# A new set of planning tables for a gated Fourier-mix and squared-ReLU MLP kernel

## Chip, cores and metric

The kernel runs on one core of a Trainium2 chip. The metric is the device time of one launch in microseconds (us). The median of three runs of the kernel before is 1730.49 us (1730.0 to 1730.5).

## What is computed

With x of 2048 rows and 1024 columns, the reference is, cut to its core:

```
g = sigmoid((x * gate_w).sum(-1, keepdims=True))
a = x @ Wd_re.T ;  b = x @ Wd_im.T                # hidden DFT, 1024 x 1024
y = Ws_re @ a - Ws_im @ b                         # sequence DFT, 2048 x 2048
h = x @ w1 + b1 ; h = where(h > 0, h, 0) ; h = h * h   # 1024 -> 3584
o = h @ w2 + b2                                   # 3584 -> 1024
out = g * y + (1 - g) * o
```

All of it is in float32.

## The kernel before

**Products.** Each of the large products is cut by a seven-product scheme (Strassen's in Winograd's form): sums of blocks ("S1" to "S4" of the left operand, "T1" to "T4" of the right, tables `SUMS_L`, `SUMS_R` and their kin) go in, seven smaller products come out, and their results are added up. For most of the seven the scheme is applied a second time (`twice`); the rest run as they are (`direct`). Each float32 operand is split into a high part `hi`, which ScalarE (ACT) writes by a copy, and a low remainder `lo`, which VectorE (DVE) writes by a subtraction; a block product is three matmuls, `hi*hi`, `lo*hi` and `hi*lo`. Narrow right operands keep both parts in one tile called `both`.

**Stages.** `x_stage` makes a and b (tiles `ab`), `c_stage` the sequence DFT (tiles `y`, stored in `gy` or in `out`), `h_stage` twice the hidden layer (tiles `h`, sums of them stored under the names `T`), `o_stage` the second layer, the gate and the last addition (tiles `o`). Sums of blocks are made by DVE (tiles `sum`, or in place in a loaded `raw` tile), or by an adding DMA from the POOL queue (`accum_op=ADD`), as the tables `LAND_*` say; `lo` can also be made by an adding DMA from a negated copy (`minus`, tables `MINUS_*`), and stored operands can be fetched again (`LOW`, `HIGH`: stores `lo<-lo`, `hi<-hi` by POOL, loads of the same names by SP).

**PSUM.** A `Group` owns one or two of four pools of PSUM, each a tile `ps` of 128 x 2 x 512 float32. In `x_stage` each block product is 24 matmuls: twelve into one pool, twelve into the next. After them DVE adds the pool's contents to a tile `ab` (an eviction), and the pool can be written again. The second-level order of the products in `twice` of a `wide` stage is

```
late = TURNS >> (0 if not flip else flip) & 1
...
if late:
    order = (1, chain), (5, other), (6, chain), (3, other), (7, chain), (2, last), (4, chain)
else:
    order = (*(begin if steps and "T1" not in ontos else begin[::-1]), (3, other), (6, chain), (2, last),
             (7, chain), (4, chain))
```

where `chain`, `other` and `last` are the groups that a product is accumulated in, and bit 0 of `TURNS` is for `x_stage`.

**Order.** The functions above only record operations. `plan` then gives each a due time by its table of costs, hands out 55 slots of SBUF (512 KB each) by due time less a lead (`LEAD`, and per 25 us of due time `LEADS`), and writes one order per engine: PE in program order, the others by due time as the planner expects them to be ready. `PATIENT` lets a POOL DMA be held back behind a later instruction (`op.gate`). `emit` issues the operations in that order; line 1628, where it does so, is the line of nearly every row of the profile. The gate's sixteen row sums (`Gate`, DVE `raw<-raw,gwb`) are placed by `GATE`, relative to the first step of `c_stage`.

Of the kernel before, what the change touches and what calls it, by code (L numbers as in the profile page):

```python
# [4 lines left out]

# [11 lines left out]
S, D, F = 2048, 1024, 3584
NF = F // P
SLOTS = 55
WIDE, TALL_C, TALL_O = (1, 2, 5, 6, 3, 7, 4), (1, 2, 5, 6, 3, 7, 4), (1, 2, 5, 6, 3, 7, 4)  # L20
WIDE_H = ((1, 2, 5, 6, 3, 7, 4), (1, 2, 5, 6, 3, 7, 4))
TWICE_X, TWICE_C, TWICE_O = (2, 3, 4, 5), {1: 4, 2: 4, 3: 4, 4: 4, 5: 2, 6: 1}, {1: 2, 2: 3, 3: 3, 4: 3, 5: 3, 7: 1}
FIRST_C, FIRST_O = {5: 2}, {7: 2}
WARM = 44
FAR_TALL, FAR_WIDE = ("T2",), ()
LAND_X, LAND_C, LAND_H, LAND_O = {'T1': 3, 'T3': 4, 'T4': 3}, {'T1': 15, 'T3': 0, 'T4': 13}, ({'T1': 0, 'T3': 4, 'T4': 3}, {'T1': 0, 'T3': 1, 'T4': 1}), {'T1': 10, 'T3': 3, 'T4': 9}
SHARE = ("S1", "S2", "S3", "S4")
NEAR_O = ("T1",)
ADD_O = range(13)
GATE, ROWS = (-44, 1), (14, 11)  # L30
OLD_X, OLD_H = (2, 6, 4), ((3, 4, 7, 6), (6, 4, 2))
SHARE2 = {1: 7, 2: 11, 3: 15, 4: 4, 5: 8, 6: 2, 7: 2}
LOW, HIGH = ({1: 111, 2: 49, 3: 109, 4: 119, 5: 32, 6: 63, 7: 36}, {1: 35, 2: 27, 3: 125, 4: 100, 5: 76, 6: 101, 7: 56}), ({1: 78, 2: 4, 3: 4, 5: 16, 6: 9, 7: 78}, {1: 33, 2: 50, 3: 41, 4: 67, 5: 4, 6: 101, 7: 19})
SPILL, LAND_CL = (1, 0), {'S1': 0, 'S2': 0, 'S3': 0, 'S4': 5}
# [24 lines left out]
ADD, SUB = ALU.add, ALU.subtract

# [9 lines left out]
LESS, LESS_C = {2: 1, 3: 1, 4: -1, 6: -1}, {2: -1, 3: -1, 4: 1, 6: -1}  # L70
# [9 lines left out]
def gated_mix_kernel(ctx: ExitStack, tc: tile.TileContext, x4, xn, w4, ct, w1a, w1b, w2, b1, b2, gw, out):  # L80
# [930 lines left out]
    def wide(left, right, rows, order, second, target, final, sign=1, onto_old=(), flip=False, lands={},  # L1011
# [143 lines left out]
    def x_stage():  # L1155
# [17 lines left out]
        def spill(c, k, near=None, lent=False):  # L1173
# [5 lines left out]
            if near is not None:  # L1179
# [136 lines left out]
    def o_stage():  # L1316
# [141 lines left out]
def plan(ops, count, start):  # L1458

    t = start  # L1460
# [32 lines left out]
    events, now, order = [], 0.0, []  # L1493
# [97 lines left out]
    while events:  # L1591
        now, _, _, what = heappop(events)
# [88 lines left out]
```

## Time and profile before

| what | value |
|---|---|
| median of three runs | 1730.49 us |
| profiled execution, first to last instruction (span) | 1727.9 us |
| PE busy | 1722.6 us (100%) |
| PE weight loads busy | 1508.7 us (87%) |
| DVE busy | 1658.3 us (96%) |
| ACT busy | 1151.2 us (67%) |
| POOL busy | 284.3 us (16%) |
| DMA: bytes, mean rate | 559.89 MB, 324 GB/s |

The profile gives the span of one execution, and no whole time of its own for it; the median of the runs is 2.6 us above the span. Busy times overlap: an engine with a share of 100% never rests, and one with less costs nothing by its rests as long as no other engine waits for it. Matmul starts are measured, their ends are modelled. As nearly all instructions have line 1628, groups are told apart by their tile names (`lo<-raw,hi` writes a `lo` tile from a `raw` and a `hi`).

### The profile page before, as it was taken

What the parts mean: (1) busy time and instruction counts of PE and PEld (TensorE: products, weight loads), DVE (VectorE), ACT (ScalarE), POOL (GpSimd) and SP (SyncE); (2) the same over time, 40 slices, a digit from 0 to 9 for tenths busy, and PEclk for the clock granted to TensorE, in tenths of its full rate; (3) what the DMA queues carried; (4) which work ended last, traced back from release to release, by engine and by line L of the source; (5) the groups of instructions that cost most, each with busy time, mean ns of one, the idle gap of its engine ahead of it and who ended that gap; (6) DMA issues with size and microseconds to landing.
All of it is one profiled execution on the core that took longest, in us unless ns stands there. A gap on an engine that the chain in (4) does not pass through costs nothing.

```text
span 1727.9 us, 22479 instructions
## 1 busy us (share of the span) xinstructions
PE 1722.6 (100%) x8024; PEld 1508.7 (87%) x8024; DVE 1658.3 (96%) x1659; ACT 1151.2 (67%) x1296; POOL 284.3 (16%) x413
## 2 busy tenths in 40 slices
PE   9999999999999999999999999999999999999999
PEld 8888888888888888888888888888888888888888
DVE  7999999999999899899999999999999999899997
ACT  5475565874675675466595668987897666476673
POOL 1212221111211100121121210101211120111131
PEclk9999999999999999999999999999999999999999
DMA  9996999999999999998998999999999999999997
GB/s 347 365 375 259 322 387 343 292 285 327 285 307 352 291 310 399 323 295 285 371 359 311 276 355 344 351 379 358 309 345 324 336 272 381 341 277 334 334 295 162
DMA packets 157807, 559.89 MB, mean 324 GB/s; under 512 B 17776, under 2 KB 18304, under 8 KB 157696
## 3 DMA queue, kind: packets, MB, share of 16 engines
q1 hardware_dynamic: 98352, 351.07, 52.9%
q0 software_dynamic: 58912, 207.00, 44.4%
q8 instruction: 63, 1.03, 0.2%
q10 hardware_dynamic: 432, 0.39, 0.1%
q14 instruction: 48, 0.39, 0.1%
HBM read 390.09 MB, written 134.75 MB: 304 GB/s over the span
## 4 chain that ended last, share of the span: by engine, by line
PE 96%; DVE 3%; DMA 1%; issue 0%; ACT 0%; DVEq 0%; POOLq 0%
PE ps L1628 96%; DVE lo L1628 1%; DVE sum L1628 1%; DMA raw<-in_w1a 1%; DVE y L1628 0%; DVE both L1628 0%; DVE u L1628 0%; DVE raw L1628 0%; ACT hi L1628 0%; ACT y L1628 0%; DVE o L1628 0%; ACT both L1628 0%; ACT ps L1628 0%; DVE ones L1628 0%; DVEq L1628 0%
## 5 line engine op out<-in xcount | busy, mean ns | idle before, releaser
L1628 PE MATMUL ps<-hi,lo 128*128 128x512 f32 (+1 forms) x2100 | 730.4, 378 | 0.1
L1628 PE MATMUL ps<-hi 128*128 128x512 f32 (+1 forms) x2100 | 730.4, 378 | 0.0
L1628 PE MATMUL ps<-lo,hi 128*128 128x512 f32 (+1 forms) x2100 | 730.3, 378 | 0.0
L1628 ACT ACTIVATE hi<-raw 128x1024 fp32r<-128x1024 f32 (+2 forms) x397 | 401.5, 1032 | 200.2 <-DVE raw L1628 79.6
L1628 PEld LDWEIGHTS ps<-hi,lo 128*128 128x128 f32 x2100 | 396.6, 189 | 56.5 <-DVE lo L1628 0.7
L1628 PEld LDWEIGHTS ps<-lo,hi 128*128 128x128 f32 x2100 | 396.7, 189 | 56.1 <-DVE lo L1628 0.2
L1628 PEld LDWEIGHTS ps<-hi 128*128 128x128 f32 x2100 | 396.6, 189 | 56.0 <-ACT hi L1628 0.2
L1628 DVE TENSOR_TENSOR lo<-raw,hi 128x1024 fp32r<-128x1024 f32 (+2 forms) x337 | 396.0, 1192 | 14.2 <-ACT hi L1628 10.8
L1628 ACT ACTIVATE hi<-sum 128x1024 fp32r<-128x1024 f32 (+1 forms) x263 | 269.1, 1032 | 136.7 <-DVE sum L1628 88.1
L1628 PE MATMUL ps<-hi,both 128*128 128x512 f32 x1120 | 312.3, 379 | 0.0
L1628 DVE TENSOR_TENSOR lo<-sum,hi 128x1024 fp32r<-128x1024 f32 (+1 forms) x230 | 270.5, 1191 | 8.7 <-PE ps L1628 4.6
L1628 PEld LDWEIGHTS ps<-hi,both 128*128 128x128 f32 x1120 | 211.7, 189 | 30.2 <-ACT ps L1628 0.2
L1628 DVE TENSOR_TENSOR raw<-raw 128x1024 f32<-128x1024 f32 (+1 forms) x175 | 205.7, 1195 | 1.6 <-DMA raw<-in_ct 0.5
L1628 DVE TENSOR_TENSOR sum<-raw 128x1024 f32<-128x1024 f32 (+2 forms) x182 | 180.5, 1002 | 7.9 <-PE ps L1628 4.4
L1628 PE MATMUL ps<-lo,both 128*128 128x512 f32 x560 | 182.9, 379 | 0.0
L1628 DVE TENSOR_TENSOR sum<-raw,sum 128x1024 f32<-128x1024 f32 (+2 forms) x139 | 147.6, 1066 | 4.4 <-DMA raw<-copy 2.1
L1628 ACT ACTIVATE u<-ps 128x1024 f32<-128x1024 f32 (+1 forms) x91 | 88.1, 970 | 47.5 <-PE ps L1628 28.0
L1628 PEld LDWEIGHTS ps<-lo,both 128*128 128x128 f32 x560 | 105.8, 189 | 15.0
L1628 ACT ACTIVATE ps<-u 128x1024 f32<-128x1024 f32 (+1 forms) x69 | 67.8, 987 | 21.9 <-DVE u L1628 9.5
L1628 POOL DMA_DIRECT2D h<-h x58 | 31.3, 542 | 250.5 <-ACT h L1628 91.0
L1628 POOL DMA_DIRECT2D lo<-raw x38 | 34.0, 896 | 224.9 <-ACT lo L1628 172.1
L1628 ACT ACTIVATE both<-sum 128x512 fp32r<-128x512 f32 x68 | 42.3, 622 | 35.9 <-DVE sum L1628 33.7
(87 smaller groups left out, 1140.0 us busy)
## 6 DMA issues: line engine op xcount, KB each, us to landing
raw<-in_ct SPq DMA_DIRECT2D x137, 512.0 KB, 10.1
raw<-h SPq DMA_DIRECT2D x99, 512.0 KB, 10.5
raw<-in_w SPq DMA_DIRECT2D x90, 512.0 KB, 10.3
raw<-ab SPq DMA_DIRECT2D x72, 512.0 KB, 10.9
raw<-copy SPq DMA_DIRECT2D x65, 512.0 KB, 7.8
raw<-in_x SPq DMA_DIRECT2D x56, 512.0 KB, 8.4
copy<-raw POOLq DMA_DIRECT2D x48, 512.0 KB, 6.9
h<-h POOLq DMA_DIRECT2D x44, 512.0 KB, 6.6
```

What stands on the lines that cost most here:

```text
L1628: made = getattr(real[op.engine], op.name)(*(actual(a) for a in op.args), **{k: actual(v) for k, v in op.kwargs.items()})
```

## The change

The arithmetic functions are the same. New are the values of the tables that decide which sums an adding DMA makes, which operands are stored and fetched, where the gate's sums stand, and how early a slot is handed out; and the planner's event heap now breaks ties by a counter instead of by an object's address. Cut to what is spoken of (a long table is cut in its line, at "..."):

```
-LAND_X, LAND_C, LAND_H, LAND_O = {'T1': 3, 'T3': 4, 'T4': 3}, {'T1': 15, 'T3': 0, 'T4': 13}, ...
+LAND_X = {'T1': 3, 'T3': 2, 'T4': 3}
+LAND_C = {'T1': 16, 'T3': 1, 'T4': 13}
...
-GATE, ROWS = (-44, 1), (14, 11)
+GATE = (-39, 1)
+ROWS = (14, 13)
...
-LOW, HIGH = ({1: 111, 2: 49, 3: 109, ...
+LOW = ({1: 47, 2: 49, 3: 109, 4: 119, 5: 32, 6: 63, 7: 36}, {1: 35, 2: 27, 3: 125, 4: 102, 5: 76, 6: 101, 7: 58})
...
-MINUS_C, MINUS_O = {1: 4227074, 2: 24661, ...
+MINUS_C = {1: 4227074, 2: 1610637397, 3: 30694026, 4: 285213248, 5: 151060480, 6: 59966531, 7: 2532114496}
...
-HIGH_FIRST, BEGIN2, TURNS, SPREAD = 26, 1, 7, 1
+HIGH_FIRST = 26
+BEGIN2 = 1
+TURNS = 6
+SPREAD = 1
...
-LEADS = {'hi': {3: -5.5, 4: -4.5, 7: 2.0, 10: 1.5, ...
+LEADS = {'hi': {1: -8.5, 2: 14.0, 3: 2.0, 4: -0.5, 5: -3.5, ...
...
+    turn = count_up()
+
     def push(t, *what):
-        heappush(events, (t, len(events) + 1e-9 * len(order), id(what), what))
+        heappush(events, (t, next(turn), 0, what))
```

By engine the built programs hold: PE 7,980 float32 matmuls in both; DVE one instruction more than before; ACT three fewer; plain loads and stores from SP and ACT 686 before and 687 now; DMAs from POOL 409 and 407, of them 169 and 166 adding ones.

**First place: PE in `x_stage`.** `TURNS` = 6 clears the bit of `x_stage`. The rows below are the first matmul of each run of twelve, from the 205th to the 277th float32 matmul; `ps_N` is a pool of PSUM in use by one group. Before:

```order
L1628 MATMUL ps_934<-hi_635,hi_645 128x512
...
L1628 MATMUL ps_954<-hi_731,hi_703 128x512
...
L1628 MATMUL ps_975<-hi_731,hi_703 128x512
...
L1628 MATMUL ps_905<-hi_759,hi_713 128x512
...
L1628 MATMUL ps_934<-hi_759,hi_713 128x512
...
L1628 MATMUL ps_954<-hi_751,hi_796 128x512
...
L1628 MATMUL ps_975<-hi_751,hi_796 128x512
```

Now:

```order
L1672 MATMUL ps_931<-hi_635,hi_646 128x512
...
L1672 MATMUL ps_950<-hi_765,hi_754 128x512
...
L1672 MATMUL ps_968<-hi_765,hi_754 128x512
...
L1672 MATMUL ps_950<-hi_700,hi_788 128x512
...
L1672 MATMUL ps_968<-hi_700,hi_788 128x512
...
L1672 MATMUL ps_906<-hi_743,hi_775 128x512
...
L1672 MATMUL ps_931<-hi_743,hi_775 128x512
```

Before, two pairs of pools take turns; now the pair `ps_950`, `ps_968` is written again as soon as its first product is done (at the 241st and the 253rd matmul). The same is new at the 337th, 349th, 505th, 517th, 877th, 1225th and 1237th: nine matmuls wait for an eviction that has twelve matmuls' time. Outside the 241st to the 1248th matmul PE's order is as it was.

**DVE at the same place.** The rows run from the eviction of the pool written before that pair. Before:

```order
L1628 TENSOR_TENSOR ab_959<-u_695,ps_934 128x1024
L1628 TENSOR_TENSOR lo_966<-sum_922,hi_944 128x1024
L1628 TENSOR_TENSOR lo_973<-raw_600,hi_956 128x1024
L1628 TENSOR_TENSOR ab_983<-u_804,ps_954 128x1024
L1628 TENSOR_TENSOR raw_864<-raw_864,raw_870 128x1024
L1628 TENSOR_TENSOR ab_1004<-u_826,ps_975 128x1024
L1628 TENSOR_TENSOR lo_1015<-raw_840,hi_988 128x1024
```

Now:

```order
L1672 TENSOR_TENSOR ab_957<-u_692,ps_931 128x1024
L1672 TENSOR_TENSOR sum_964<-raw_778,raw_790 128x1024
L1672 TENSOR_TENSOR ab_973<-u_811,ps_950 128x1024
L1672 TENSOR_TENSOR sum_983<-raw_624,raw_829 128x1024
L1672 TENSOR_TENSOR ab_997<-u_841,ps_968 128x1024
L1672 TENSOR_TENSOR lo_1006<-sum_964,hi_977 128x1024
L1672 TENSOR_TENSOR lo_1013<-sum_983,hi_1002 128x1024
```

One instruction instead of two stands ahead of the eviction of the pair's first pool; one stands between the two evictions, as before.

**Second place: POOL at the change from `c_stage` to `h_stage`.** An adding DMA onto a tile `raw` from `in_w1a`, and the stores behind it. Before:

```order
L1628 DMA raw_7183<-in_w1a 128x1024 [waits DMAHW4_49,DMASW0_49,DMAHW5_49,DVE_49,Activation_49]
L1628 DMA copy_426<-sum_7386 128x1024 [waits DMASW1_49,Activation_49]
L1628 DMA hi_428<-hi_7396 128x1024 [waits DMASW2_49,Activation_49]
L1628 DMA lo_427<-lo_7417 128x1024 [waits DMASW3_49]
L1628 DMA copy_429<-sum_7462 128x1024 [waits DMASW4_49,DVE_49]
```

Now:

```order
L1672 DMA raw_7167<-in_w1a 128x1024 [waits DMASW6_49,DMAHW4_49,DVE_49,Activation_49]
L1672 DMA copy_424<-sum_7385 128x1024 [waits DMASW7_49,DVE_49]
L1672 DMA hi_426<-hi_7396 128x1024 [waits DMASW0_49,Activation_49]
L1672 DMA lo_425<-lo_7417 128x1024 [waits DMASW1_49]
L1672 DMA copy_427<-sum_7463 128x1024 [waits DMASW2_49,DVE_49]
```

The order of the five is the same. What moved is what the third waits for: before, the store of `hi_7396` was held until a later ACT copy (the one that writes `hi` from the `raw` tile of `copy_364`) was done; now it waits for its own tile alone. The store of `lo` behind it comes free with it.

## Rows read from the trace of the kernel before

**Rows 1.** The page: span, and busy time with share and count by engine.

```profile
span 1727.9 us, 22479 instructions
PE 1722.6 (100%) x8024; PEld 1508.7 (87%) x8024; DVE 1658.3 (96%) x1659; ACT 1151.2 (67%) x1296; POOL 284.3 (16%) x413
PEclk9999999999999999999999999999999999999999
```

**Rows 2.** Windows of 50 us: PE, PEld, DVE, ACT, POOL busy (count), PEclk, DMA share, GB/s.

```profile
50.00:100.00 50.00, 50.00 (x234) 43.77 (x233) 48.60 (x48) 22.72 (x23) 8.22 (x14) 1.00 1.03 373
100.00:150.00 50.00, 50.00 (x234) 43.77 (x233) 50.00 (x49) 35.00 (x38) 9.04 (x17) 1.00 0.82 322
...
800.00:850.00 50.00, 49.85 (x231) 43.36 (x230) 48.94 (x44) 35.58 (x37) 7.76 (x12) 1.00 0.96 334
```

**Rows 3.** Groups by form: count | busy us, mean ns | idle before.

```profile
L1628 PE MATMUL ps<-hi,lo 128*128 128x512 f32 x2084 | 726.7, 379 | 0.1
L1628 PE MATMUL ps<-hi,both 128*128 128x512 f32 x1120 | 312.3, 379 | 0.0
L1628 PE MATMUL ps<-lo,both 128*128 128x512 f32 x560 | 182.9, 379 | 0.0
L1628 PE MATMUL ps<-hi 128*128 128x256 f32 x16 | 3.9, 274 | 0.0
L1628 PEld LDWEIGHTS ps<-hi,lo 128*128 128x128 f32 x2100 | 396.6, 189 | 56.5 <-DVE lo L1628 0.7
```

**Rows 4.** Timeline of PE: start, duration (us), instruction; first matmul, one stretch, last.

```profile
5.69 0.70 PE L1628 MATMUL ps<-hi 128*128 128x512 f32 x2
...
54.81 0.38 PE L1628 MATMUL ps<-hi,lo 128*128 128x512 f32 x1
55.03 0.38 PE L1628 MATMUL ps<-hi 128*128 128x512 f32 x1
...
1723.57 0.28 PE L1628 MATMUL ps<-hi,lo 128*128 128x256 f32 x1
```

**Rows 5.** Timeline of PE around 827 us.

```profile
827.16 0.38 PE L1628 MATMUL ps<-lo,hi 128*128 128x512 f32 x1
827.69 0.48 PE L1628 MATMUL ps<-hi,lo 128*128 128x512 f32 x1
828.01 0.38 PE L1628 MATMUL ps<-hi 128*128 128x512 f32 x1
```

**Rows 6.** Timeline of DVE in `x_stage`; in brackets idle time before, and its releaser.

```profile
53.08 1.21 DVE L1628 TENSOR_TENSOR ab<-u,ps 128x1024 f32<-128x1024 f32 x1
55.69 1.23 DVE L1628 TENSOR_TENSOR lo<-sum,hi 128x1024 fp32r<-128x1024 f32 x1 [1.40 <-ACT hi L1628]
...
57.97 1.22 DVE L1628 TENSOR_TENSOR ab<-u,ps 128x1024 f32<-128x1024 f32 x1
...
84.07 1.21 DVE L1628 TENSOR_TENSOR ab<-u,ps 128x1024 f32<-128x1024 f32 x1
```

**Rows 7.** The chain that ended last, in order of time, ahead of 827.69 us.

```profile
815.91 9.39 DMA raw<-in_w1a
...
825.32 1.06 ACT hi L1628
...
826.41 1.24 DVE lo L1628
827.64 0.04 issue
```

**Rows 8.** Timeline of POOL, 814 to 830 us.

```profile
817.48 0.57 POOL L1628 DMA_DIRECT2D copy<-sum  x1 [0.66 <-ACT hi L1628]
829.51 0.53 POOL L1628 DMA_DIRECT2D hi<-hi  x1 [11.46 <-ACT hi L1628]
```

**Rows 9.** Window 810 to 820 us: columns as in the windows above.

```profile
810.00:820.00 10.00, 10.00 (x48) 8.77 (x47) 10.00 (x10) 8.87 (x11) 1.48 (x2) 1.00 1.00 350
```

**Rows 10.** Timeline of DVE: its last instruction.

```profile
1724.40 0.43 DVE L1628 TENSOR_TENSOR o<-o,raw 128x256 f32<-128x256 f32 x1
```

More of the change, by code (lines that the diff above doesn't have):

```diff
@@ L3 @@
 from heapq import heappop, heappush
-from itertools import cycle, zip_longest
+from itertools import count as count_up, cycle, zip_longest
 import concourse.bass as bass
@@ L16 @@
 P = 128
[L17 removed]
+S = 2048
+D = 1024
+F = 3584
 NF = F // P
 SLOTS = 55
[L20 removed]
+WIDE = (1, 2, 5, 6, 3, 7, 4)
+TALL_C = (1, 2, 5, 6, 3, 7, 4)
+TALL_O = (1, 2, 5, 6, 3, 7, 4)
 WIDE_H = ((1, 2, 5, 6, 3, 7, 4), (1, 2, 5, 6, 3, 7, 4))
[L22 to L25 removed]
@@ L26 @@
-LAND_X, LAND_C, LAND_H, LAND_O = {'T1': 3, 'T3': 4, 'T4': 3}, {'T1': 15, 'T3': 0, 'T4': 13}, ({'T1': 0, 'T3': 4, 'T4': 3}, {'T1': 0, 'T3': 1, 'T4': 1}), {'T1': 10, 'T3': 3, 'T4': 9}
+TWICE_X = (2, 3, 4, 5)
+TWICE_C = {1: 4, 2: 4, 3: 4, 4: 4, 5: 2, 6: 1}
+TWICE_O = {1: 2, 2: 3, 3: 3, 4: 3, 5: 3, 7: 1}
+FIRST_C = {5: 2}
+FIRST_O = {7: 2}
+WARM = 44
+FAR_TALL = ("T2",)
+FAR_WIDE = ()
+LAND_X = {'T1': 3, 'T3': 2, 'T4': 3}
+LAND_C = {'T1': 16, 'T3': 1, 'T4': 13}
+LAND_H = ({'T1': 0, 'T3': 4, 'T4': 4}, {'T1': 0, 'T3': 1, 'T4': 3})
@@ L27 @@
+LAND_O = {'T1': 10, 'T3': 3, 'T4': 9}
 SHARE = ("S1", "S2", "S3", "S4")
 NEAR_O = ("T1",)
-ADD_O = range(13)
-GATE, ROWS = (-44, 1), (14, 11)
[L31 to L34, printed above, removed]
@@ L36 @@
-MADE = {'T1': 6884, 'T3': 14556}
-TWICE_H = ((1, 2, 5, 3, 4, 6, 7), (1, 2, 5, 3, 4, 6))
-MM, MM_END, FIRST_MM = 0.2157, 0.18, 6.2
-VEC, VEC_END, ACT, ACT_END = (0.07, 1.0417e-3), 0.39, (0.09, 0.843e-3, 0.04, 0.095), 0.41
-ADDING = 0.85, 2.1, 2.2
-ISSUE, RING, RATE, SEM, LANES = {'gpsimd': 0.56, 'scalar': 0.36, 'sync': 0.36}, {'gpsimd': (1.6, 1.6), 'scalar': (1.8, 1.8), 'sync': (1.8, 1.8)}, (420000.0, 395000.0), 0.06, 8
+ADD_O = range(0, 14)
+GATE = (-39, 1)
+ROWS = (14, 13)
+OLD_X = (2, 6, 4)
+OLD_H = ((3, 4, 7, 6), (6, 4, 2))
@@ new lines @@
+LAND2_H = ({1: ('T3',), 2: ('T3',), 3: ('T3',), 4: ('T1',), 5: ('T1',), 6: ('T1',), 7: ('T1',)}, {1: (), 2: (), 3: (), 4: (), 5: (), 6: ('T3', 'T1'), 7: ('T3', 'T1')})
+LAND2_O = {1: {'T1': 1, 'T3': 0}, 2: {'T1': 1}, 3: {'T3': 3}, 4: {'T3': 1}, 5: {'T1': 3, 'T3': 2}, 6: {'T1': 2}, 7: {'T1': 3, 'T3': 4}}
+MADE = {'T1': 6884, 'T3': 14552}
+TWICE_H = ((1, 2, 5, 3, 4, 6, 7), (1, 2, 5, 3, 4, 6))
+MM = 0.2157
+MM_END = 0.18
+FIRST_MM = 6.2
+VEC = (0.07, 1.0417e-3)
+VEC_END = 0.39
+ACT = (0.09, 0.843e-3, 0.04, 0.095)
@@ L43 @@
+ACT_END = 0.41
+ADDING = 0.85, 2.1, 2.2
+ISSUE = {'gpsimd': 0.56, 'scalar': 0.36, 'sync': 0.36}
+RING = {'gpsimd': (1.6, 1.6), 'scalar': (1.8, 1.8), 'sync': (1.8, 1.8)}
+RATE = (420000.0, 395000.0)
+SEM = 0.06
+LANES = 8
 RUN = {768: 0.75, 512: 0.6}
-EARLY_C, EARLY_O = 17172, 47911
+EARLY_C = 19120
+EARLY_O = 45373
 SQUARE = ((), ())
-NOW_C, NOW_O = (384, 17152, 12816), (12930, 4736, 6144)
-APART_C, APART_O = (640, 63815), (35458, 26362)
-MINUS_C, MINUS_O = {1: 4227074, 2: 24661, 3: 30694026, 4: 16777792, 5: 151060480, 6: 26936387, 7: 116195392}, {1: 205653010, 2: 8983296, 3: 67907648, 4: 93114368, 5: 42107932, 6: 243963922, 7: 30949506}
@@ L56 @@
+MINUS_O = {1: 232914962, 2: 67703552, 3: 67907648, 4: 76042496, 5: 42106904, 6: 243963922, 7: 155992194}
+RELU = ((), (3,))
+TWINS_C = 1
+TWINS_O = 3
+BOTH_C = 20720
+BOTH_O = 6718
+HIGH_FIRST = 26
+BEGIN2 = 1
+TURNS = 6
+SPREAD = 1
+BY_ROW_C = 251
+BY_ROW_O = 56
+BEGIN = 1
+OUT = 15
+NOT_OUT = ((0, 0, 1, 0), (0, 1, 0, 0), (0, 1, 1, 1), (1, 0, 1, 0), (1, 1, 0, 1), (1, 1, 1, 0))
+LATE = 720.0
+PATIENT = (32.0, 0)
 LEAD = {'hi': 2.2, 'out': 1.4, 'raw': 6.7, 'sum': 10.0}
-LEADS = {'hi': {3: -5.5, 4: -4.5, 7: 2.0, 10: 1.5, 11: -1.0, 15: -3.0, 16: -6.0, 18: 2.0, 19: 5.5, 20: 7.5, 25: -0.5, 29: -4.5, 30: -9.5, 31: -2.5, 37: 4.5, 38: -0.5, 40: -1.0, 41: 3.5, 42: 2.5, 43: -3.0, 44: -7.0, 45: 1.0, 47: 0.5, 50: -1.0, 54: -5.0, 61: -1.0, 62: -2.0, 64: -2.0}, 'out': {9: -2.0, 12: 3.0, 15: -3.0, 17: -1.5, 25: 5.5, 34: -2.0, 41: -0.5, 45: 2.0, 49: -8.0, 55: 3.0, 56: 6.5, 65: 4.0}, 'raw': {3: -1.0, 10: 2.0, 11: -2.0, 13: 1.0, 14: 4.5, 16: 1.5, 17: 4.5, 18: 7.5, 19: 7.5, 25: 5.0, 29: -5.5, 33: 0.5, 35: 4.0, 36: -1.0, 39: 1.0, 40: -2.0, 41: -0.5, 42: 1.5, 43: 2.0, 48: -2.0, 50: -1.0, 51: 3.0, 56: 4.0, 61: -3.5, 63: 1.5, 64: -2.5}}
@@ L63 @@
+ADD = ALU.add
+SUB = ALU.subtract
 SUMS_L = {"S1": ((1, 0), (1, 1), SUB), "S2": ((0, 0), "S1", SUB), "S3": ((1, 0), (0, 0), SUB),
```

21 lines of the change are left out of this document (13 added, 8 removed).

## Prediction

> **What bounds the kernel now.** I read the page first. PE is busy for 1722.6 of 1727.9 us, DVE for 96%, and the granted clock is at 2.4 GHz throughout (PEclk 9 in all 40 slices, 1.00 in the windows) [rows 1, 2]. A busy PE is not yet a PE at its limit, since matmul ends are modelled, so I looked next at the distance between matmul starts. The timeline shows 0.216 us from one start to the next [rows 4], and the windows hold 234 matmuls in 50 us; the one from 800 us holds 231 [rows 2]. The groups by form count the matmuls: 3 x 2084 + 1120 + 560 = 7932 of 512 columns and 3 x 16 = 48 of 256 [rows 3]. The first starts at 5.69 us; 7932 x 0.216 = 1713.3, and 48 at half of that add 5.2: the last would end near 1724.2. It ends at 1723.57 + 0.28 = 1723.85 [rows 4]. So the whole span is a run-up of 5.7, an unbroken row of matmuls, and a tail on DVE and the output DMA of 4.0 us [rows 10]. The reader should see that nothing is left between the matmuls, except at one place: the matmul after the one at 827.16 starts at 827.69 instead of 827.38, and the next 0.10 late: 0.42 us in all [rows 5].
>
> The chain of waits names what that place waits for: an adding DMA onto `raw` from `in_w1a` issued at 815.91, 9.39 us to land, then ACT's `hi`, DVE's `lo`, and PE 0.04 us after [rows 7]. That is the only time in the stream that a better plan can win. The 5.7 us ahead and the 4.0 behind hang on the first loads and the last products, and the first and the last dozen of each queue's rows that serve them stand as they did.
>
> **The change part by part.** *Amounts.* PE has the same matmuls. DVE has one instruction more, 1.2 us like those in [rows 6], beside the 70 us in which it rests: nothing on the path. Three adding DMAs fewer, one store and one load more: one 512 KB transfer less among some 1100, beside PE. None of these can shorten a stream that PE fills; they matter only where they make an operand late. The other moved tables (sums, fetches, slots, the gate's sums five steps later) go with these: cover is PE's own stream, which hides them as long as each operand lands before its matmul. If one does not, its lateness adds to the time in full, because PE has no rest in which to catch up.
>
> *The nine evictions in x_stage.* This is the term that I can price. With two pairs of PSUM pools in turn, a pool has 36 matmuls, 7.8 us, between its last matmul and its next writer. At nine places it now has 12. Take the first. The 228th matmul, the last into its pool, starts at 54.81 [rows 4] and is done by 55.19. The 241st is due 13 x 0.216 = 2.81 us after that start, at 57.62. DVE's addition takes 1.21 [rows 6] and PE follows 0.04 us after DVE [rows 7], so the eviction must begin by 56.37, 1.18 us after the pool is done. In the trace the eviction of that pool began at 57.97 [rows 6], 2.78 us after. It cost nothing there, since the pool was not wanted before 62.8. Begun at the same time now, it holds PE until 59.22: a wait of 1.60. Near the second place the row at 84.07 reads the pool of the 348th matmul, which is done at 54.81 + 120 x 0.216 + 0.38 = 81.11; that is 2.96 us late, or a wait of 1.78 if nothing had been waited before. DVE is full here (48.6 and 50.0 of 50 us, [rows 2]), so its lateness against PE stays about the same, and what PE has waited once it does not wait again: the pair costs its largest wait, not the sum.
>
> Against this, the order now has one DVE instruction ahead of that eviction where it had two. From 55.69 to 57.97 two of them took 2.28 [rows 6], so one is 1.14; that much less gives a lateness of 1.64 and a wait of 0.46. The places at the 877th matmul and after lie where DVE is again on time or nearly, and I cost them at nothing; if that cover is gone, one of them is worth the same wait as here. Bounds for the stage: 0 (DVE in time, as it was at 53.08, with the gate's sums out of the way) and 5.4 (three visits at 1.78 each, below). I take 1.2, between 0.46 and 1.78 and nearer the upper, as DVE is the fuller the later it gets.
>
> *The adding DMA at 816 us.* Its place in POOL's order is the same, so the 0.42 us remain. New is that two stores of 512 KB behind it, which before were held until 829.51 [rows 8], now go about 11 us sooner and share the DMA engines while it flies. The window moves 350 GB/s with the engines full [rows 9], so 512 KB are 1.5 us of it. Bounds: 0 (they queue behind it) and 3.0 (they take their full share first); the adding DMA cannot land sooner by this. I take 0.4, near the lower end, since one such store, at 817.48, already flew with it [rows 8] and it still landed in 9.39.
>
> *The gain.* If the moved slots bring every load in time, the 0.42 us go. I do not count it, as the chain that makes them is unchanged.
>
> **The sum.** 1727.9 + 1.2 + 0.4 = 1729.5 us of span, against the profiled execution's own 1727.9. That execution's span lies 2.6 below the median of 1730.49; with the same 2.6 around it the time is 1732.1 us. A measurement of this kernel can tell about 0.2%, 3.5 us, from no change; the forecast lies within that.
>
> **The rivals.**
>
> *All is hidden.* DVE is never more than 1.18 us late at the nine places, and the adding DMA lands in time: 1730.49 - 0.42 = 1730.1, or 1730.5 with that wait kept. For it: DVE was on time at 53.08 [rows 6], and the sums of the gate that filled it now come later. Against it: 1.40 us of waiting for ACT were enough to make it 2.78 late two instructions on [rows 6].
>
> *Slower: every visit pays anew.* The nine places make five visits; three lie in the stretch where DVE is full. PE's wait lets DVE catch up, but between the visits, some 20 and 35 us apart, DVE falls behind again, as it did from 53.08 to 57.97. Then each visit costs up to 1.78: 5.3 to 5.4 us, 1735.9. It decides from 3.5 us on, that is from two full visits. For it speaks that a full DVE stays late; against it that it takes a wait to fall behind, and those are few.
> The Trainium skill, page "Perfetto Trace Analysis", section "Optimizing Tensor Performance", Matmuls, says that independent groups should rotate through PSUM banks so that one group's evacuation overlaps the next one's matmuls. The trace before agrees, as an eviction 2.78 us late cost PE nothing; by that rule the change, which gives up the rotation at nine places, would be slower, and this rival is its mechanism.
>
> *The stores delay the adding DMA.* The full 3.0 us beside the 1.2: 1730.49 + 4.2 = 1734.7. For it: the engines are full in that window [rows 9]. Against it: the stores are issued after it on the same queue.
>
> *Faster: the stream is not at its limit.* Weight loads are busy for only 87% [rows 1]. If the other 13%, 219 us, were slack that a better order could use, a fiftieth of it would be 4.4 us: 1726.1. But a weight load of 189 ns [rows 3] goes with each start of 0.216 us, which is 87.5%, in an unbroken stream too.
> The Trainium skill, same page, section "Identifying the Most-Contended Engine", says that weight-load busy share, not matmul busy time, measures how near PE is to its limit; read so, 13% would be open here. The rows speak against that reading: the starts are evenly spaced at full clock.
>
> That the change does not do what it says is seen from the counts: DVE gets no relief, one instruction more, so no gain hangs on that.
>
> **How the numbers follow.** Forecast (waits of 0.5 to 3.4 us in all) 0.55; all hidden 0.25; every visit pays 0.13; stores delay the adding DMA 0.05; faster 0.02. Of the fourth, 0.03 lies over the bound and 0.02 under it. Slower by over 0.2%: 0.13 + 0.03 = 0.16; faster 0.02; within 0.2%: 0.82. The range goes from 1729.6 (all hidden, less the 0.5 by which runs of the kernel before differ) to 1735.0, which takes in half of each slower rival, so that about one in ten is left out above.
>
> **What would show it.** In the trace of the changed kernel PE's starts around 57.6 us should show a gap of 0.5 to 1.8, released by DVE `ab`, with little added at 79 and 115 us; windows of 50 us from 300 us on should again be without a gap but for that around 827 us; the adding DMA from `in_w1a` should land in 9 to 11 us with a gap of 0.4 to 0.8 after it. No gap at 58 us would make the first term wrong; gaps at three or more visits would make the slower rival right. A gap at a place that I have not named, in `c_stage` or `o_stage`, would mean that a load which I cost at nothing came late, and the sum would be wrong by that gap.

## The result, and the profile after

The changed kernel takes 1735.28 us (median of six runs, 1734.12 to 1738.16) against 1730.05 (1729.79 to 1730.5) for the kernel before: a ratio of 1.0031, 95% interval 1.0020 to 1.0043. It is slower by 5.2 us; the forecast was 1732.1 us, and the time lies just above its range. Its runs spread over 4.0 us, those of the kernel before over 0.7. The profiled execution took 1735.3 us, its span is 1733.4.

The page of the changed kernel, as [rows 1], and the waits of its PE:

```profile
span 1733.4 us, 22475 instructions
PE 1723.9 (99%) x8024; PEld 1507.7 (87%) x8024; DVE 1658.4 (96%) x1660; ACT 1150.6 (66%) x1293; POOL 281.4 (16%) x411
PEclk9999999999999999999999999999999999999999
```

```profile
engine line waited for: us in total, times, longest us
PE ps L1672 <- DVE ab L1672: 1.6, 1, 1.6
PE ps L1672 <- ACT ps L1672: 1.5, 1, 1.5
PE ps L1672 <- DVE ones L1672: 1.1, 1, 1.1
PE ps L1672 <- ACT hi L1672: 0.6, 1, 0.6
PE ps L1672 <- DVE both L1672: 0.5, 1, 0.5
PE ps L1672 <- DVE lo L1672: 0.2, 1, 0.2
```

Work and clock are as before: no engine's busy time differs by more than 3 us. In the kernel before, the same view has the wait for `ones` alone. What changed is the distance of PE's starts. Measured at 0.216 us a start, and adding up every excess of over 0.1 us (the start behind a gap is most often 0.10 late too), the trace before has 0.42 us of gaps [rows 5], the trace after 5.84. Its last matmul starts at 1729.22, 5.65 later than before [rows 4]. Where they stand (start, duration, in brackets the idle time and its releaser; PE's timeline of the changed kernel):

```profile
57.61 0.38 PE L1672 MATMUL ps<-hi,lo 128*128 128x512 f32 x1
59.58 0.48 PE L1672 MATMUL ps<-hi 128*128 128x512 f32 x1 [1.59 <-DVE ab L1672]
...
393.58 0.38 PE L1672 MATMUL ps<-hi,both 128*128 128x512 f32 x1
395.44 0.48 PE L1672 MATMUL ps<-hi,both 128*128 128x512 f32 x1 [1.48 <-ACT ps L1672]
...
1428.08 0.48 PE L1672 MATMUL ps<-hi,both 128*128 128x512 f32 x1 [0.49 <-DVE both L1672]
...
1702.89 0.48 PE L1672 MATMUL ps<-lo,hi 128*128 128x512 f32 x1 [0.22 <-DVE lo L1672]
```

59.58 - 57.61 - 0.216 = 1.75, and 0.10 more at the next start: 1.86 in all, unrounded, at the first of the nine places in x_stage. In the same way 1.75 at 395 us, 0.60 near 515, 0.76 at 1428, 0.88 at 1703 to 1709. None of the other eight places of x_stage shows one in this trace, and the 0.42 near 827 are gone. 1733.4 - 5.84 and 1727.9 - 0.42 give 1727.6 and 1727.5: the gaps, and a first matmul that starts 0.19 us later, are the whole difference.

Why PE waits there is seen on DVE. Of its waits for loads and for PE, some of the largest rows, before and after:

```profile
DVE sum L1628 <- PE ps L1628: 8.5, 9, 3.1
...
DVE lo L1628 <- PE ps L1628: 7.0, 6, 2.2
...
DVE sum L1628 <- DMA raw<-copy: 3.1, 4, 1.8
...
DVE sum L1628 <- DMA raw<-in_x: 1.2, 1, 1.2
```

```profile
DVE raw L1672 <- DMA raw<-in_w: 5.4, 4, 3.3
DVE raw L1672 <- DMA raw<-in_x: 5.0, 2, 4.7
DVE sum L1672 <- DMA raw<-copy: 4.5, 4, 2.5
DVE lo L1672 <- PE ps L1672: 4.3, 5, 2.1
...
DVE raw L1672 <- DMA raw<-h: 3.0, 1, 3.0
```

All rows on DMA sum to 6.5 us before and 24.8 after, all on PE and its sequencer to 33.6 and 18.0. Before, most of this rest was for PE, and DVE was ahead; now most of it is for DMAs, and after such a rest DVE can be behind. The longest rest for a load ends some 10 us ahead of the first gap. DVE's timeline of the changed kernel:

```profile
49.22 1.22 DVE L1672 TENSOR_TENSOR raw<-raw 128x1024 f32<-128x1024 f32 x1 [4.72 <-DMA raw<-in_x]
...
58.32 1.21 DVE L1672 TENSOR_TENSOR ab<-u,ps 128x1024 f32<-128x1024 f32 x1
```

From 49.22 to 58.32 DVE does eight instructions without a pause, then the eviction, which ends at 59.53; PE goes on at 59.58. The four loads from in_x were issued from 32.87 us on, after SP had waited 11.9 us in its queue; the view of SP's waits, 20 to 33 us, names a `sum` of DVE (I take it for the last reader of the slot that the first of them is given; the view doesn't say so):

```profile
SPq L1672 <- DVE sum L1672: 11.9, 1, 11.9
```

### The profile page after: what moved, and what is told of

Its sections match the earlier page's. It is cut to its first block, busy times and chain, and to the rows that moved or that the text cites. A ratio compares the mean times of both kernels' runs of the same rounds, so it can differ in the third digit from the quotient of the medians.

```text
span 1733.4 us, 22475 instructions
## 1 busy us (share of the span) xinstructions
PE 1723.9 (99%) x8024; PEld 1507.7 (87%) x8024; DVE 1658.4 (96%) x1660; ACT 1150.6 (66%) x1293; POOL 281.4 (16%) x411
## 3 DMA queue, kind: packets, MB, share of 16 engines
q0 software_dynamic: 58496, 205.95, 43.8%
## 4 chain that ended last, share of the span: by engine, by line
PE 75%; DVE 2%; issue 0%; ACT 0%; DVEq 0%
PE ps L1672 75%; DVE lo L1672 1%; DVE u L1672 0%; DVE o L1672 0%; DVE sum L1672 0%; DVE y L1672 0%; ACT ps L1672 0%; DVE both L1672 0%; DVEq L1672 0%
## 5 line engine op out<-in xcount | busy, mean ns | idle before, releaser
L1672 DVE TENSOR_TENSOR lo<-raw,hi 128x1024 fp32r<-128x1024 f32 (+2 forms) x339 | 397.9, 1190 | 17.1 <-ACT hi L1672 13.6
```

Source lines behind the costliest of these rows:

```text
L1672: made = getattr(real[op.engine], op.name)(*(actual(a) for a in op.args), **{k: actual(v) for k, v in op.kwargs.items()})
```

## The experiments

**One table put back.** TURNS at 7, then LEADS of the kernel before, each in the changed kernel. The planner makes a whole new order for each.

```
-TURNS = 6
+TURNS = 7
```
```
-LEADS = {'hi': {1: -8.5, 2: 14.0, ...
+LEADS = {'hi': {3: -5.5, 4: -4.5, ...
```

> The change with TURNS back at 7, so that the two pairs of PSUM pools take turns in x_stage again; all other tables new. Theory (the gap of 1.75 + 0.10 us at 59.6 us is the eviction that has twelve matmuls' time where it had 36): that gap goes, the gaps at 395, 515, 1428 and 1703 to 1709 us stay, and the time is 1735.3 - 1.85 = 1733.4 us. Rival (DVE is late there because a load from in_x came 4.7 us late, and it stays late with any order of the pools): the gap only moves to a later place of x_stage or is added to the one at 395 us, and the time stays at 1735.3 within 0.5.

> The change with the table LEADS (slot lead times per 25 us) of the kernel before; all other tables new. Theory (the new tables of the stages put DVE's instructions in another order, and DVE reaches the evictions late for that; the leads are secondary): gaps of 3 us and more in all remain, and the time is 1733.5 to 1737. Rival (the new leads bring slots and so loads late, and DVE late with them): DVE's waits for DMAs and the gaps at 395, 515 and 1428 us go, and the time is 1730.5 to 1732.5, with at most the gap near 59 us left.

Measured: 1748.61 us (ratio 1.0107, 1.0091 to 1.0123) and 1761.47 (1.0185, 1.0168 to 1.0202). With TURNS at 7 the first gap of the trace stands at 392.75 us: in x_stage the theory held. But there are 16.0 us of gaps in all, most of them at places that neither theory had. With the old LEADS there are 30.5 us, 6.60 of them ahead of the start at 1339.62; both theories failed, since what they shared, that a table can be put back by itself, is not so here.

**The tables of one stage put back** in the changed kernel: the eight of c_stage, then the seven of o_stage, for instance

```
-BOTH_C = 20720
+BOTH_C = 17904
```
```
-BOTH_O = 6718
+BOTH_O = 7998
```

> The change with the eight tables of c_stage (LAND_C, LAND2_C, EARLY_C, NOW_C, APART_C, MINUS_C, BOTH_C, BY_ROW_C) of the kernel before; all else new. The order up to some 300 us is that of the changed kernel, so the gap of 1.85 at 59.6 us must stay. Theory (the gaps of c_stage belong to its own tables): the 1.74 at 395 and the 0.59 at 515 us go, and the time is 1735.3 - 2.3 = 1733.0. Rival (they come from the leads or from DVE's backlog out of x_stage): a gap of 1 to 2 us remains near 395 us, and the time is 1734.5 to 1736.

> The change with the seven tables of o_stage (ADD_O, LAND2_O, EARLY_O, NOW_O, APART_O, MINUS_O, BOTH_O) of the kernel before; all else new. The order is that of the changed kernel up to some 1100 us, so the gaps at 59.6, 395 and 515 us (1.85 + 1.74 + 0.59) must stay; that they come again at the same places also tells how steady they are. Theory (the gaps of o_stage belong to its own tables): the 0.66 at 1428 and the 0.86 at 1703 to 1709 us go, and the time is 1735.3 - 1.5 = 1733.8. Rival (they come from the leads): 1735.3 within 0.5.

Measured: 1747.81 (1.0099, 1.0082 to 1.0115) and 1737.63 (1.0042, 1.0028 to 1.0057). With the old tables of c_stage 0.56 are left near 395 and 0.35 near 513, but after 1200 us there are some 12 us of gaps. In its trace every queue has the order of the change up to 405 us, so the smaller gap near 395 is no effect of the tables: PE had waited 1.44 at 59 us and 0.87 at 273 already. With those of o_stage the gaps at 1428 and 1703 us are gone, as expected; 0.42 near 1319 and 0.58 near 1460 are new. The time rose all the same. In the traced execution, the slowest of the four, this is seen in x_stage: in the same order the gap near 59 us was longer, the clock fell after it, and 0.73 came up at 275 us. PE, and windows (us: PE, PEld, DVE, ACT, POOL, PEclk, DMA share, GB/s):

```profile
60.71 0.48 PE L1672 MATMUL ps<-hi 128*128 128x512 f32 x1 [2.47 <-DVE ab L1672]
...
61.59 0.63 PE L1672 MATMUL ps<-hi 128*128 128x512 f32 x1
62.02 0.63 PE L1672 MATMUL ps<-lo,hi 128*128 128x512 f32 x1
```

```profile
60.00:62.00 2.00, 1.29 (x4) 1.08 (x5) 2.00 (x3) 1.80 (x3) 0.55 (x1) 0.83 1.06 283
62.00:64.00 2.00, 2.00 (x6) 1.62 (x5) 2.00 (x3) 0.88 (x1) 0.00 (x0) 0.50 1.03 295
64.00:66.00 2.00, 2.00 (x9) 1.66 (x9) 1.90 (x3) 0.00 (x0) 0.53 (x1) 0.82 1.03 408
```

After 2.85 us from start to start the granted clock is 0.50 (1.2 GHz) for seven starts of 0.43 us each: the gap of 2.64 costs 1.6 more.

**Plan kept, a few instructions moved.** From here on the order of the changed kernel is left as `plan` made it, slots included, and single instructions are put behind a later one. Near 55 us, then near 385, then both and one at 1427, this one with the POOL store of its result (DVE's rows):

```
 ab_934<-u_679,ps_906
-raw_829<-raw_829,raw_834
-raw_850,z_238<-raw_850,gwb_637
 ab_957<-u_692,ps_931
 sum_964<-raw_778,raw_790
 ab_973<-u_811,ps_950
-sum_983<-raw_624,raw_829
+raw_829<-raw_829,raw_834
 ab_997<-u_841,ps_968
+raw_850,z_238<-raw_850,gwb_637
+sum_983<-raw_624,raw_829
...
-lo_3744<-sum_3710,hi_3728
 sum_3754<-raw_3258,sum_3437
-lo_3763<-raw_3607,hi_3750
...
 y_3795<-y_3795,ps_3507
+lo_3744<-sum_3710,hi_3728
+lo_3763<-raw_3607,hi_3750
...
-raw_12689<-raw_12689,raw_12199
 both_12871<-sum_12857,both_12871
+raw_12689<-raw_12689,raw_12199
```

> The changed kernel with its plan kept and three of DVE's instructions put a few places later near 55 us: the addition of raw_829 behind the eviction ab_973, the gate's row sum and sum_983 behind the eviction ab_997. Every other queue is as it was. Theory (the gap at 59.6 us is DVE reaching that eviction late, after 4.7 us of waiting for a load from in_x and with two instructions ahead that could wait): the evictions begin at about 56.0 and 58.3 us, no gap is left near 59 us, and the time is 1735.3 - 1.85 = 1733.4 us, with runs closer together. Rival (DVE has no room, and what it saves here it owes at the next place): the 1.85 come back between 60 and 400 us, and the time is 1735.3 within 0.5.

> The changed kernel with its plan kept and two of DVE's instructions put later near 385 us: lo_3744 and lo_3763 (wanted by PE at about 402 and 405 us in this kernel's time) behind the six that make y and free the PSUM pool for ACT's ps. Theory (the gap of 1.74 at 395.4 us is DVE's order alone): the six end 2.28 us sooner, ACT's ps with them, that gap is gone, and the time is 1735.3 - 1.74 = 1733.6 us. Rival (the two lo then come late, or ACT's ps waits for something else): a gap of 0.5 us or more near 395 to 406 us, and 1735 us.

> The moves of the two runs above together, and at 1427 us one addition of raw tiles (and the store of its result) put behind the both tile that PE waits for. Theory (each gap is local: DVE's order there decides it): 1.85 + 1.74 + 0.66 = 4.25 us go, the gaps at 515 and 1703 to 1709 us (1.4 in all) stay, and the time is 1731.0 us. Rival (DVE's backlog is carried on, and PE's gain of 3.6 us makes it late again): the gaps at 515 and 1703 us grow, and the time stays over 1733 us.

Measured: 1735.63 (1.0035, 1.0024 to 1.0046), 1736.42 (1.0045, 1.0028 to 1.0062), 1734.49 (1.0028, 1.0016 to 1.0040). The times are nearer those of the rivals. Each gap went from its place, and the time did not: in the first run 1.39 us came up at the next place where a pair of pools is used again at once, in the third 2.07 at 80.34, 0.96 at 273.07, 1.00 at 468.32 and 1.54 near 516. The traces have 3.6, 6.1 and 7.2 us of gaps in all; the first is of the fastest of its seven executions. In the second run the gap that its rival names, at 395 to 406 us, did not come.

```profile
78.22 0.38 PE L1701 MATMUL ps<-hi,lo 128*128 128x512 f32 x1
79.72 0.48 PE L1701 MATMUL ps<-hi 128*128 128x512 f32 x1 [1.12 <-DVE ab L1701]
```

In x_stage DVE's lateness was not made by the order at the gap, so another order there does not remove it. At 1428 us the one move was enough: the third trace has no gap there.

**TURNS alone, in the kernel before.** The one-line change of above, the other way round.

> The kernel before with TURNS at 6, the first term of the prediction by itself; the planner makes a new order for it, which can add waits of its own. Theory (the reduced turn of the PSUM pools costs what DVE is late at the first of the nine places, once): a gap of 1.2 to 1.8 us near 59 us, none at the other eight, so 1730.05 + 1.5 = 1731.5 us if the new plan is as good elsewhere. Rival (any new plan that was not searched for runs into gaps far from x_stage): over 1735 us, with the larger part of it after 300 us.

Measured: 1743.12 (1.0078, 1.0063 to 1.0093). A gap of 0.72 at 58.11, none at the other eight places, and 12.7 us after 390: the rival. The place in x_stage is real, smaller than expected, and hidden under the new plan's cost.

**The change once more, and the load's wait taken out.** First the changed kernel unaltered. Then one instruction moved: the addition that waits for the load goes behind two that are ready sooner.

```
-raw_790<-raw_790,raw_802
 lo_914<-sum_856,hi_897
 lo_923<-raw_576,hi_908
+raw_790<-raw_790,raw_802
 ab_934<-u_679,ps_906
```

> The changed kernel once more, unaltered, for a second trace of it on the chip of the runs beside it. If its gaps belong to the plan, they stand again at 59.6, 395, 515, 1428 and 1703 us with nearly the same lengths. If they come from loads that land at other times in every execution, the place of 59.6 stays but its length moves by 0.5 us or more, and of the others some are gone and some are elsewhere; the time is 1734 to 1738 us in either case.

> The changed kernel with one instruction of DVE moved: the addition raw_790 (which waits for a load from in_x, 4.7 us of idle DVE at 44.5 to 49.2 us) is put behind lo_914 and lo_923, which have what they need by 47.0 and 48.5. DVE then does two instructions, 2.28 us, inside the idle stretch, less what it waits for ACT in it, so it is 1.8 us earlier at the eviction. Theory (the gap at 59 us is this idle time, handed on by a full DVE): the eviction ab_973 begins near 56.5, the gap at 59 us shrinks from 1.85 to 0 to 0.3, and, other than when the evictions were only put ahead of other work, no gap of over 0.4 us comes up at 79 us; the profiled span falls by 1.5 to 1.85 against the unaltered run beside it. Rival (the order of DVE at the eviction is what counts, whatever it waited for): the gap stays at 59 us within 0.5, or comes back at 79 us at over 1 us.

Measured: 1735.65 (1.0037, 1.0024 to 1.0049) and 1734.36 (1.0027, 1.0017 to 1.0037). The second trace of the change has 5.94 us of gaps: 2.10 at 59.68, 1.44 at 273.50, 0.10 at 395, 0.24 each near 515 and 1359, 0.90 at 1428, 0.91 from 1702.90 on. So those at 59, 1428 and 1703 belong to the plan. The one at 273 is new, and it is no gap of c_stage: it stands at the 1225th matmul, the eighth of the nine places, and is released by an eviction. The traces with the old tables of c_stage and of o_stage, whose order is the same up to there, show 0.87 and 0.73 at this matmul.

```profile
273.50 0.48 PE L1672 MATMUL ps<-hi 128*128 128x512 f32 x1 [1.17 <-DVE ab L1672]
```

Ahead of it DVE waited 2.88 us at 162 us (for a store) and 2.04 at 205 (for ACT's `hi`), where it waited 1.83 and less than 0.4 in the first trace. Up to 396 us both traces have 3.6 us of gaps, at different places: what PE had waited at 273 it did not wait again at 395.

The gap at 59 us follows the load. Five traces share the order up to there (the two of the change, the old tables of c_stage, those of o_stage, and the one moved at 385 us). In them the addition that waits for the load begins at 49.22, 49.32, 49.24, 50.35 and 49.35 us, and the eviction at 58.32, 58.41, 58.34, 59.45 and 58.44: 9.09 or 9.10 later in each.

With the addition moved, DVE's two waits there are 0.95 and 2.82 us instead of 0.78 and 3.94, and it does ready work while the load flies:

```profile
47.84 1.23 DVE L1701 TENSOR_TENSOR lo<-sum,hi 128x1024 fp32r<-128x1024 f32 x1 [2.82 <-PE ps L1701]
48.98 1.22 DVE L1701 TENSOR_TENSOR lo<-raw,hi 128x1024 fp32r<-128x1024 f32 x1
50.12 1.22 DVE L1701 TENSOR_TENSOR raw<-raw 128x1024 f32<-128x1024 f32 x1
...
56.93 1.22 DVE L1701 TENSOR_TENSOR ab<-u,ps 128x1024 f32<-128x1024 f32 x1
```

The eviction begins 1.4 us sooner than in the first trace of the change, the gap at 58.20 is 0.38, and nothing comes up at 79 us: here most of the lateness itself is gone. A gap of 1.17 stands at 271.75, the 1225th matmul again. The trace has 4.2 us of gaps, and its span is 1731.9 against 1733.4. The medians differ by 1.3 us and their intervals overlap, so the gain is shown by the traces and not by the times.

**Without the gate's sums.**

```
+if "accum_out" in op.kwargs:
+    made = tc.nc.vector.tensor_copy(actual(op.kwargs["accum_out"]), actual(op.args[1])[:, :1])
```

> The changed kernel without its sixteen row sums of the gate: in their places DVE copies one column instead, so that 16 x 1.15 = 18 us of DVE's work, nearly all of it between 39 and 136 us, is left out; all else, the order of every queue too, is as it was. Theory (in x_stage PE pays for a DVE that has no room): of the gaps ahead of 300 us at most 0.7 us is left at 59 us (one sum of 1.15 us stood ahead of that eviction), and nothing at 79; the gaps in c_stage and o_stage, where no sum of the gate stands, stay in number and sum (2 to 4 us). Rival (the reduced turn of the PSUM pools alone makes the gap): 1.2 us or more at 59 us.

Measured: 1734.76 (1.0028, 1.0018 to 1.0039). No gap between 7 and 270 us, 0.26 at 270.46 (the 1225th matmul), and 3.7 us after it, in c_stage and o_stage. So the theory holds: the shorter turn of the pools costs only where DVE has no room. The median is not clear of that of the change.

**The new tables of o_stage in the kernel before.**

> The kernel before with the seven new tables of o_stage (ADD_O, LAND2_O, EARLY_O, NOW_O, APART_O, MINUS_O, BOTH_O); its order is that of the kernel before up to some 1100 us. Theory (the new tables of o_stage put more of DVE's work ahead of 1430 and 1705 us, where it then has no rest left): no gap before 1100 us but the 0.42 near 827, gaps of 1 us and more in all after it, with DVE's waits for loads up from 0.8 us after 1340 us to several, so 1731 us or more. Rival (the new leads did it, and the tables are free): no gap after 1100 us, and 1730.0 within 0.5.

Measured: 1734.37 (1.0025, 1.0015 to 1.0035; runs 1732.03 to 1736.97). Up to 1100 us the trace, one of the two fastest of eight, has 0.33 us of gaps, then 2.00 at 1317 to 1319 and 0.33 at 1425, the matmul of the change's gap at 1428. So the new tables cost with the old leads too, mostly at another place; whether the tables do it or the new order that the planner made of them isn't told apart. The run has the new tie-break of the event heap too, and in its trace every queue has the order of the kernel before up to 1128 us: up to there the tie-break changes nothing. DVE's waits for loads after 1340 us rose only from 0.8 to 1.7 us, where I had expected several.

**DVE made late, in the kernel before**, by repeating one of its instructions, in x_stage (three times more) and in o_stage (five times more):

```
+for _ in range(3 if op is slow else 0):
+    made = getattr(real[op.engine], op.name)(...)
```

> The kernel before with one of DVE's instructions in x_stage (lo_907, at 48.5 us) done four times in a row instead of once: 3.4 us more of DVE's work at this place, nothing else changed. It makes DVE about as late in x_stage as the changed kernel's wait for a load does, but the pools of PSUM take turns. Theory (the turn of 36 matmuls is the room in which DVE may be late): 1.4 of the 3.4 us go into the idle time at 54.3 us, the eviction of 57.97 begins near 60, its pool is not wanted before 62.8, and PE loses nothing in x_stage: 1729.9 within 0.4. Rival (DVE has no room there, and all lateness is paid somewhere): gaps of 1.5 us and more between 55 and 300 us, 1731.5 or more.

> The kernel before with one of DVE's instructions in o_stage (lo_14425, at 1602 us) done six times in a row instead of once: 5.7 us more of DVE's work there, nothing else changed. DVE rests 3.1 us between 1600 and 1705 us in the kernel before (0.5 in the changed one, which has gaps of 0.9 in all at 1703 to 1709 us). Theory (PE pays for DVE's work beyond its rests): 5.7 less some 2.5 of those rests leaves DVE 3 us later than before near 1700 us, 2 us later than in the changed kernel, and gaps of 1.5 to 3.5 us in all stand between 1605 and 1710 us: 1731.5 to 1733.5 us. Rival (DVE's lo and both tiles are made long before they are wanted): no gap over 0.2, and 1729.9 within 0.4.

Measured: 1730.61 (1.0005, 0.9996 to 1.0014) and 1736.03 (1.0034, 1.0021 to 1.0046). By the traces the repeats took 3.8 and 6.3 us. In x_stage they cost one gap of 0.36 us behind the start, at 126.03, though the eviction began at 60.00, 2.03 later than in [rows 6] and later than in either trace of the change: the pools' turn is the room, as expected (the median is 0.7 us higher, the interval takes in no change). In o_stage the repeats, done by 1608.5 us, cost 6.1:

```profile
1621.38 0.48 PE L1635 MATMUL ps<-hi 128*128 128x512 f32 x1 [1.57 <-ACT ps L1635]
...
1626.62 0.48 PE L1635 MATMUL ps<-hi 128*128 128x512 f32 x1 [2.38 <-ACT ps L1635]
```

```profile
1626.00:1628.00 2.00, 1.38 (x5) 1.22 (x6) 2.00 (x3) 1.92 (x3) 0.12 (x1) 0.86 1.07 326
1628.00:1630.00 2.00, 2.00 (x6) 1.55 (x6) 2.00 (x3) 0.65 (x1) 0.00 (x0) 0.50 1.07 276
```

1.84 and 2.64 us of gaps, and 1.6 by the clock that fell after the second. The theory's direction holds, but not its size: PE paid 13 to 18 us after the extra work. The gaps are 1.8 us less than it, where I had counted on rests of 2.5, and the clock adds 1.6.

**Seven instructions moved** in the changed kernel (the expectations count eight): those at 45, 385 and 1427 us as above, and two at 159 and 203 us.

```
-lo_1809<-sum_1787,hi_1796
 ab_1819<-ab_1478,ps_1678
 lo_1829<-sum_1724,hi_1802
+lo_1809<-sum_1787,hi_1796
...
-lo_2142<-raw_1974,hi_2127
 raw_2031<-raw_2031,raw_2034
 raw_2049<-raw_2049,raw_2052
+lo_2142<-raw_1974,hi_2127
```

> The changed kernel with its plan kept and eight instructions moved: the addition that waits for the load from in_x behind two lo (as in the run that did this alone); lo_1809 behind an eviction and a lo at 159 us, where DVE waited 1.8 to 2.9 us; lo_2142 behind two additions of raw tiles at 203 us, where it waited 2.0 for ACT; the two lo at 385 us behind the six that make y; and at 1427 us one addition of raw tiles and its store behind the both tile that PE waits for. Theory (PE pays for what DVE waits, wherever the next instruction without room stands): with DVE's waits ahead of 300 us down by 4 us and more, the gaps at 59, 272 and 395 us are under 0.4 each, what is left is 0.3 to 1.0 at 515 and 0.66 at 1703 to 1709 us, and the time is 1731 to 1732.5 us. Rival (the gaps only move on, as with the evictions put ahead at 55 and 385 us): the sum of the gaps stays over 4 us, and the time over 1733.5.

> The kernel with the eight moved instructions once more, for a second trace, since its times spread over 6.7 us while the traced execution, the fastest of seven, had only 2.9 us of gaps. Theory (what DVE waits differs from one execution to the next, and PE pays the difference): if this execution is slower than 1733.5 us, its gaps sum to over 4 us, stand at other places than 270, 465, 513 and 1700 us, and DVE's waits for loads or ACT ahead of them are longer than in the first trace. Rival (the traced execution was like the others, and the time lies outside PE's stream): gaps of about 2.9 us again, whatever the time.

> The same kernel a third time, to the same end: a slower execution should show more and longer gaps, and longer waits of DVE ahead of them; a fast one (1732 to 1733 us) should look like the first trace.

Measured: 1734.92 (1.0029, 1.0018 to 1.0040; 1732.18 to 1738.84), 1732.94 and 1734.34. By the traces the first theory holds: in all three no gap over 0.43 us at 59, 272, 395 and 1428 us, and 2.8, 3.2 and 4.6 us of gaps with spans of 1730.3, 1731.1 and 1732.5. By the median it does not, as 1734.92 is hardly below the unaltered change. What the third trace loses stands elsewhere (1.10 at 466.23 and 0.95 at 820.08). That DVE waits longer in it is so ahead of these two places only (1.15 us at 369.55, 0.57 and 0.46 in the others; 1.27 at 796.50, under 0.4 in the others): in all, its waits for DMAs and ACT are 45.4, 44.8 and 43.8 us. The 0.9 at 1700 us stand in all three, as in both traces of the change. So repaired places stay repaired, but the plan has more of them than these. No version here beats the kernel before.

## Why the prediction was wrong

*What bounds the kernel.* Right: the stream of PE, and nothing else. Span less gaps is 1727.4 to 1727.8 in the traces of both kernels and of the runs with extra work.

*Amounts and moved tables at nothing.* This is the step that failed: "cover is PE's own stream, which hides them as long as each operand lands before its matmul", and with it that one instruction more on DVE is "nothing on the path" beside the 70 us in which it rests. The operand is made by DVE, and DVE is busy for 96%. Its rests are not a reserve that can be drawn on anywhere: from one place where it is ahead of PE to the next matmul without room, it has only the rests that lie between. Gaps at places that I had not named, costed at nothing, are 1.75 + 0.60 + 0.76 + 0.88 = 3.99 us in the first trace of the change, and 0.10 + 0.24 + 0.24 + 0.90 + 0.91 = 2.39 in the second.

The runs show two ways in which DVE comes late. One is a late load, as at 59 us, where in five traces the eviction follows the addition that waited for the load by the same 9.1 us. The other is more work in a stretch, without a late load. At 1338 and at 1522 us DVE of the changed kernel is ahead, as it waits for PE, the second time by way of ACT's `u`:

```profile
1338.27 0.69 DVE L1672 TENSOR_TENSOR sum<-raw,sum 128x512 f32<-128x512 f32 x1 [0.89 <-PE ps L1672]
```

```profile
1521.19 1.02 ACT L1672 ACTIVATE u<-ps 128x1024 f32<-128x1024 f32 x1 [2.31 <-PE ps L1672]
```

```profile
1522.24 1.22 DVE L1672 TENSOR_TENSOR o<-o,ps 128x1024 f32<-128x1024 f32 x1 [1.73 <-ACT u L1672]
```

From there to the gaps at 1428 and 1703 us it waits for no load and hardly rests. DVE in the second of these stretches, before and after (us, DVE's busy time and count, PEclk, DMA share, GB/s):

```profile
1516.00:1697.00 181.00, 176.34 (x180) 1.00 1.01 305
```

```profile
1521.00:1702.00 181.00, 178.66 (x182) 1.00 0.99 302
```

In the first it is busy for 83.4 of 86 us before and 85.4 after, again with two instructions more. So the 9.1 us of rests for loads from 1458 to 1516 us, over a third of the 24.8, cost nothing, and the gaps at 1428 and 1703 are work that was moved to where DVE has no room. For 1428 a run shows it (one addition moved, no gap); for 1703 it is read from these rows, and the 6.3 us of work added to the kernel before in o_stage show the same by their 6.1.
The Trainium skill, page "Perfetto Trace Analysis", section "Identifying the Most-Contended Engine", says that for VectorE the busy share is a fair measure of how near it is to its limit. The runs agree: at the 96% of [rows 1], 6.3 us more of DVE's work in o_stage came out as 4.5 us of gaps and 6.1 us of time.

*The evictions in x_stage.* At the first place the mechanism was right, the size too small: 1.86 and 2.10 us in the two traces of the change against 1.2 taken, above the upper bound of 1.78 for one visit. The prediction's first reading, an eviction begun as late as before, gave 1.60. It began 0.35 us later (58.32 for 57.97) and PE was 0.19 later: 1.76, as measured before the next start. What did not come is the discount for one instruction less ahead of it, as 4.72 us of waiting for a load replaced 1.40 of waiting for ACT [rows 6]. That a pair costs its largest wait held. That the other visits cost nothing held in the first trace only: in the second the visit at the 1225th matmul cost 1.44, "the same wait as here", where I had counted on DVE being in time. With the first visit this is 3.5 us, where the rival in which every visit pays begins to decide; its three full visits no trace of the change shows. I also took the gate's sums, now later, as help for DVE. Without them in the change the gap at 59 us was gone: one of them stands at 54.90, in the full stretch, while DVE rests ahead of it. What their move alone does was not tried.
The Trainium skill, same page, section "Optimizing Tensor Performance", Matmuls, advises to rotate through PSUM banks so that evacuation overlaps. The runs agree: with the eviction begun at 60.00 PE lost 0.36 us in x_stage where the pools take turns, and with it begun at 58.32 it lost 1.86 where they do not.

*The adding DMA.* Wrong in sign, and small: the 0.42 us are gone in both traces of the change. The first of the two stores does go sooner now, 1.4 us behind the adding DMA instead of 13.6. The adding DMA itself was issued 4.40 us later than before and PE was as late, so the gaps ahead gave no cover. It landed sooner: ACT's `hi`, which waits for it, began 8.90 us after the issue instead of 9.41 [rows 7, 8].

```profile
820.31 0.92 POOL L1672 DMA_DIRECT2D raw<-in_w1a  x1 [7.56 <-DVE lo L1672]
...
821.74 0.57 POOL L1672 DMA_DIRECT2D hi<-hi  x1
```

```profile
829.21 1.06 ACT L1672 ACTIVATE hi<-raw 128x1024 fp32r<-128x1024 f32 x1 [0.93 <-DMA raw<-in_w1a]
```

In other traces the same distance is 8.09, 8.73 and 8.88 (x_stage made late, second trace of the change, no gate's sums), without a gap, and 9.30 and 9.65 (the addition moved, place one), with 0.36 and 0.72. So the term of 0.4 for the stores is shown by no run, and why the DMA lands sooner is open.

*Still open.* That SP's wait of 11.9 us for a slot makes the load late is read from rows; the load was not moved. What makes PE wait near 515 us was not followed up, and at 395 us only so far: ACT's `hi` waited 3.86 us for a load there and DVE 1.45 for ACT. Which of the tables moved the work in o_stage was not told apart. No run with a repaired place has a median clear of the change's own, and which places its slower executions lose by is known for two traces alone.

## What to carry to other kernels

Where a second engine is nearly as full as the one that bounds the kernel, price each moved load and each moved instruction by that engine's order: from the last place where it waited for the bounding engine to the next instruction without room. Look at whether that engine rests because it is ahead (it waits for PE) or because it is behind (it waits for a load): the same busy share hides both. A plan like this one can't be judged by its parts, as any table or stage put back alone cost 2 to 26 us more here; and of a kernel with such waits one trace shows where, and only several runs how much.

## What was not expected of the hardware

A gap can cost more than its length. After gaps of up to 2.00 us (1.75, 1.97 and 2.00 among them) the next matmuls started at full clock, 0.32 and then 0.22 apart. After those of 2.64 and 2.54 us the granted clock was 0.50 (1.2 GHz) for seven starts, which cost another 1.6 us each; in the traces with TURNS at 7 and with the old LEADS it also fell after gaps of 2.09, 2.18, 2.21 and 6.60. And loads land differently enough from one execution to the next to move PE's gaps: in one and the same order up to 300 us the eviction near 59 us began between 58.32 and 59.45, as the load landed, and the gap there was 1.34, 1.75, 2.00 and 2.64 us, the shortest where PE itself had already lost 0.42.
